# Reading a third row block's normalised input back transposed, with its layer-norm sums on ScalarE, in a linear-attention block kernel

## Chip, core and metric

The kernel runs on one NeuronCore of a Trainium2 chip. The metric is the device time of one execution in microseconds (us); smaller is better. The core has five engines that matter here: TensorE (PE in the profile, with its weight loads as PEld), VectorE (DVE), ScalarE (ACT), GpSimd (POOL) and SyncE (SP, which only issues DMAs). Each engine takes its instructions strictly in the order in which the kernel wrote them, and waits on semaphores for the others.

## What is computed

One transformer block on 2048 rows of 512 numbers, with a conditioning vector `c`:

```python
mod = (silu(c) @ w_mod).reshape(1, 6, 1, 512)
sa, ca, ga, sb, cb, gb = (mod[:, i] for i in range(6))
h = layernorm(x) * (1 + ca) + sa
q, k, v = h @ wqkv                 # 32 heads of 16
pq, pk = phi(q), phi(k)            # phi(t) = where(t > 0, t + 1, exp(t)) + 1e-6
kv, z = pk^T v, sum of pk over the rows
x = x + ga * ((pq kv) / (pq z + 1e-6)) @ wo
h = layernorm(x) * (1 + cb) + sb
x = x + gb * (mish(h @ w1 + b1) @ w2)
```

Only the first layer norm and the K products, in the first fifth of the program, are touched by the change.

## The kernel before, in words

**Tiling.** The 2048 rows are four blocks (b = 0 to 3) of four tiles (t = 0 to 3) of 128 rows by 512 columns. All tensors are float32; each product is made of three matmuls of split numbers: a tile is cut into an upper part (`...h`, type fp32r) and the rest (`...l`), and `mm3` (lines 76 to 78) multiplies upper by upper, upper by rest and rest by upper. `split` (lines 80 to 94) writes the upper part with a copy on ScalarE (line 84) or GpSimd (line 86) and the rest with a subtraction on VectorE (line 90, or 92 with a constant added).

**One block of the first stage.** Each block is loaded (`load_x`), its layer norm is taken (mean and variance per row, then `x` is normalised in place), and from then on two forms of it are used. Normalised rows, split, are `xn`. The transposed block, scaled and shifted by the modulation columns `mc` and split, is `hT` (four tiles, j = 0 to 3, of 128 columns by 512 rows). `k_unit(b, t)` multiplies `hT` of the block by the K weights into `pk`, 12 matmuls; `k_post` makes `phi` of it (`e_k` and `relu_k` on ScalarE, `ku` on VectorE) and splits that into `pk...h` (ScalarE) and `pk...l` (VectorE). `g_unit(b, t)` then adds the product of `xn` and `pk` to `gacc`, 12 matmuls. So TensorE has, for each block from b = 1, four k units and then four g units, and the next block's `hT` has to be there when the g units end.

**How hT is made.** Block 2 and block 1 go through TensorE: `transpose` (line 277) makes four transposes of 128x128 for each of the four `hT` tiles into PSUM, ScalarE scales and shifts them into `hf` (line 287), then `split`. Block 3, the only one in `TURNED`, goes through memory instead: the normalised tiles are written to DRAM (`to_dram`, line 243, on GpSimd's queue), are read back in squares of 32 rows (`load_squares`, line 256, 16 DMAs on SyncE's queue), each 128x512 tile is turned by a VectorE transpose in `turn` (line 264), and ScalarE scales and shifts it in SBUF (line 269).

**How the layer norm is made.** `ln_side` (line 487) takes the statistics of all four tiles of a block on VectorE (`bn_stats` and `bn_aggr`, lines 198 and 199), one tile per step; `ln_rstd` raises variance + eps to the power -1/2 on GpSimd (line 207); tiles 0 and 1 are then normalised on ScalarE (line 216) and tiles 2 and 3 on VectorE (line 218). A second way exists for single tiles of blocks 0 and 1: `act_sums` (line 220) gets mean and sum of squares with two ScalarE instructions that accumulate along the row (lines 228 and 229).

**The order of the work** is written by hand. The main program calls the units in TensorE's order; generators given to `spawn` are advanced one step by each `tick()`, generators given to `spawn_idle` when their turn comes, at most two a tick. What a step issues is appended to the queue of its engine at that point, and stays there. `q_right(c)` (idle work, line 386) makes the differences `qt` of blocks 0 and 1 for a later product: eight subtractions, eight upper and eight rest parts. `mod_side` multiplies modulation weights `wm` on VectorE. `tick` follows every unit, so in block 1 there are eight ticks, in block 2 eight more.

Of the kernel before, what the change touches and what calls it, by code (L numbers as in the profile page):

```python
# [11 lines left out]
ALU = mybir.AluOpType  # L12

P = 128
S = 2048
D = 512
F = 1792
NB = S // 512
NF = F // P
LAG = 3  # L20

TURNED = (3,)
SLOTS = 101
EPS = 1e-5
TINY = 1e-6
# [2 lines left out]
def block_kernel(ctx: ExitStack, tc: tile.TileContext, x, wqkv, wo, w1, b1t, w2, c, wmodt, out):  # L28
# [23 lines left out]
    def spawn(gen):  # L52
        fresh.append(iter(gen))
# [44 lines left out]
    def load_x(b, j, key="x", eng=sp):  # L98
        t = xt[key, b, j] = sb(f"{key}_{b}_{j}")
        r0 = 512 * b + P * j  # L100
        eng.dma_start(t, x[r0:r0 + P, :])
# [90 lines left out]
    def ln_stats(key, b, j, t):  # L192

        for d, name, shape in (mv, "mv", [P, 4, 2]), (rs, "rs", [P, 4]), (nb, "nb", [P, 4]):
            if (key, b) not in d:
                d[key, b] = cst.tile(shape, F32, tag=name, name=f"{name}_{key}_{b}", bufs=NB)
        st6 = cst.tile([P, 6], F32, tag="st6", name=f"st6_{key}_{b}_{j}", bufs=4)
        dve.bn_stats(st6, t)
        dve.bn_aggr(mv[key, b][:, j, :], st6)

    def ln_eps(key, b, lo=0, hi=4):
        dve.tensor_scalar(rs[key, b][:, lo:hi], mv[key, b][:, lo:hi, 1], EPS, 1.0, op0=ALU.add, op1=ALU.mult)  # L202

    def ln_rstd(key, b, lo=0, hi=4):

        y = rs[key, b][:, lo:hi]
        pool.tensor_tensor(y, y, half[:, lo:hi], op=ALU.pow)  # L207

    def ln_shift(key, b, lo=0, hi=4):

        dve.scalar_tensor_tensor(nb[key, b][:, lo:hi], mv[key, b][:, lo:hi, 0], -1.0, rs[key, b][:, lo:hi],
                                 op0=ALU.mult, op1=ALU.mult)
# [28 lines left out]

    nd, yd = {}, {}

    def to_dram(key, b, t, v):
        if (key, b) not in nd:
            nd[key, b] = drp.tile([512, D], F32, name=f"{key}d_{b}")
        pool.dma_start(nd[key, b][P * t:P * (t + 1), :], v)

    def squares(y, d, col):

# [233 lines left out]
                        plus_one(16, 20)  # L484
            yield

    def ln_side(b):
        for j in range(4):
            ln_stats("x", b, j, xt["x", b, j])
            if j == 3:  # L490
                ln_eps("x", b)
                ln_rstd("x", b)
            yield
        ln_shift("x", b)
        for j in range(4):
            t = xt["x", b, j]
            ln_apply("x", b, j, t, t, act if j < 2 else dve)
            if j % 2:
                yield
                if b in TURNED:  # L500
                    for i in (j - 1, j):
                        to_dram("x", b, i, xt["x", b, i])


    def stats(b, t):
        ln_stats("x", b, t, xt["x", b, t])
# [140 lines left out]
    apply(1, 3, act, shift=False)  # L647
    step(xsplit[3], kpost[3])
    make_constants()
    for j in range(4):  # L650
        load_x(2, j)
    g_unit(0, 2)
    spawn(ln_side(2))
    tick()
    for j in range(4):
        tr = transpose("x", 1, j, 4, 0, "h" if j < 3 else "tp", pool)
# [175 lines left out]
    for b in range(1, NB):  # L832
        last = b == NB - 1
        if b == NB - 2:
            spawn(mod_side(range(8, 12), 1))
        for t in range(4):
            k_unit(b, t)
            if b + 2 < NB:
                load_x(b + 2, t)
                if b + 2 in TURNED and t == 2:  # L840
                    spawn(ln_side(b + 2))
            if b + 1 in TURNED and t == 3:
                load_squares("x", b + 1, range(4))
            if b == NB - 2:
                load_wqkv(0, t)
            if last and t < 2:
                spawn_idle(q_left(t))
            if last and t == 2:
                spawn_idle(early_rows[0])
            xn_split(b, t)  # L850
            tick()
        if b + 2 < NB and b + 2 not in TURNED:
            spawn(ln_side(b + 2))
        if last:
            spawn(wo_scale())
        for t in range(4):
            if b + 1 in TURNED and t < 2:
                for j in (2 * t, 2 * t + 1):
                    tr = turn_x(b + 1, j)
                    next(tr)  # L860
                    spawn(tr)
            elif not last and b + 1 not in TURNED and t % 2 == 0:
                for j in (t, t + 1):
                    tr = transpose("x", b + 1, j, 4, 0, "tp" if j == t else "h")
                    next(tr)
                    spawn(tr)
            g_unit(b, t)
            if b == 1 and t == 1:
                spawn_idle(q_right(0))
            if b == 1 and t == 3:  # L870
                spawn_idle(q_right(1))
            if last:
                load_x(0, t, "r")
                for k in ((0, 1), (2,), (3,), ())[t]:
                    spawn(split(f"wq_{k}", wraw[0, k], wq, k))
                if t == 2:
                    z_unit()
                if t == 3:
                    spawn(z_side())
            if b == NB - 2:  # L880
                wv[t] = sb(f"wv_{t}")
                sp.dma_start(wv[t], wqkv[P * t:P * (t + 1), 1024:1536])
                wos[t] = sb(f"wo_{t}")
                sp.dma_start(wos[t], wo[P * t:P * (t + 1), :])
            tick()
# [669 lines left out]
```

## Time and profile before

| what | value |
| --- | --- |
| time, median of 3 runs | 485.33 us (484.69 to 486.44) |
| span of the profiled execution, first to last instruction | 483.0 us |
| what lies around the span: median less span | 2.3 us (the lowest and the highest run: 1.7 and 3.4) |
| PE busy | 477.7 us, 99% |
| DVE busy | 384.5 us, 80% |
| ACT busy | 295.7 us, 61% |
| POOL busy | 148.4 us, 31% |
| granted TensorE clock | 1.000 |

The profiled execution has no device time of its own on record apart from its span, so the 2.3 us around it come from the median of the three timed runs. In the timeline a row reads: start, duration, engine, line, operation, tiles written and read, shape, count, and in brackets how long the engine had been idle before it and what ended that. Two instructions of one engine overlap a little in their rows, so what an instruction costs its queue is the distance from its start to the next start, not its duration.

### The profile page before, as it was taken

Reading aid. Unit: us, or ns where it says so; the run is one execution under the profiler, and the core shown is the slowest. Engines: PE = TensorE matmul, PEld = TensorE weight load, DVE = VectorE, ACT = ScalarE, POOL = GpSimd, SP = SyncE. Lnnn points to the kernel's source line nnn. Section 1 sums busy time; section 2 is a strip of 40 time slices with the busy share of each in tenths; the row PEclk is TensorE's granted clock in tenths of the full one; section 3 lists DMA queues with packets and bytes.
Section 4 is the critical chain, followed back from the end, with each engine's and each line's share of the span. In section 5 each row is a group of like instructions: output and inputs, shape, how many; then the busy total and the mean of one; then the engine's idle time right before and its main releaser. Section 6 shows DMA issues by size and latency. Waiting matters only on the chain.

```text
span 483.0 us, 7291 instructions
## 1 busy us (share of the span) xinstructions
PE 477.7 (99%) x2342; PEld 393.6 (81%) x2342; DVE 384.5 (80%) x741; ACT 295.7 (61%) x528; POOL 148.4 (31%) x248
## 2 busy tenths in 40 slices
PE   8999999999999999999999999999999999999997
PEld 6788887878878888888888888888888888888887
DVE  7989989999799699977775874899644664789993
ACT  6777686866555979647676755683174454668300
POOL 4583320000022114102324434323617410243500
PEclk9999999999999999999999999999999999999999
DMA  8805599144874307389699998979999922499977
GB/s 312 299 9 127 138 160 266 51 135 150 290 196 110 121 30 263 111 284 335 216 299 350 364 251 187 321 227 340 346 363 332 291 61 62 109 181 211 240 117 167
DMA packets 121823, 101.69 MB, mean 211 GB/s; under 512 B 65937, under 2 KB 87449, under 8 KB 121786
## 3 DMA queue, kind: packets, MB, share of 16 engines
q1 hardware_dynamic: 90504, 55.47, 41.2%
q0 software_dynamic: 29024, 45.24, 37.3%
q10 hardware_dynamic: 2258, 0.53, 0.5%
q8 instruction: 18, 0.29, 0.3%
q14 instruction: 19, 0.16, 0.1%
HBM read 64.50 MB, written 34.61 MB: 205 GB/s over the span
## 4 chain that ended last, share of the span: by engine, by line
PE 93%; DVE 4%; ACT 1%; issue 1%; POOL 0%; ACTq 0%; DVEq 0%
PE p_a L1142 20%; PE p_s L1142 8%; PE oacc L78 5%; PE oacc L76 5%; PE oacc L77 5%; PE m L78 5%; PE m L77 5%; PE m L76 5%; PE o L76 3%; PE o L78 3%; PE o L77 3%; PE pq_a L409 3%; PE pk L78 2%; PE pk L76 2%; PE pk L77 2%; PE gacc L77 2%
## 5 line engine op out<-in xcount | busy, mean ns | idle before, releaser
L207 POOL TENSOR_TENSOR rs_n<-rs_n,half 128x1 f32<-128x1 f32 x16 | 11.4, 711 | 62.0 <-DVE rs_n L202 36.4
L1147 DVE TENSOR_TENSOR cb<-p_s,u 128x512 f32<-128x512 f32 x28 | 19.2, 687 | 11.6 <-ACT u L1183 10.9
L1152 ACT ACTIVATE u<-p_a 128x512 f32<-128x512 f32 x14 | 8.4, 598 | 26.2 <-PE p_a L1142 17.9
L1440 POOL DMA_DIRECT2D wt_m<-w2t x20 | 14.0, 702 | 32.9 <-PE p_a L1142 21.4
L1134 ACT ACTIVATE ub<-cb,b1c 128x512 f32<-128x512 f32 x28 | 20.0, 717 | 5.6 <-DVE cb L1147 5.4
L1177 ACT ACTIVATE u<-p_a 128x512 f32<-128x512 f32 x12 | 7.2, 599 | 24.7 <-PE p_a L1142 24.7
L1183 ACT ACTIVATE u<-p_a 128x512 f32<-128x512 f32 x14 | 8.4, 597 | 15.7 <-PE p_a L1142 15.7
L1147 DVE TENSOR_TENSOR c<-p_a,u 128x512 f32<-128x512 f32 x14 | 9.5, 688 | 8.2 <-PE p_a L1142 7.1
L900 POOL DMA_DIRECT2D rden_d<-rden x2 | 1.4, 719 | 46.5 <-DVE rden L898 46.5
L300 ACT ACTIVATE e_k<-pk 128x512 f32<-128x512 f32 x15 | 8.9, 591 | 10.8 <-PE pk L78 10.8
L779 POOL DMA_DIRECT2D w2b<-w2d x20 | 10.6, 541 | 14.5 <-DVE r L1126 4.6
L773 POOL DMA_DIRECT2D wb<-w2d x14 | 9.9, 709 | 12.4 <-DVE t L751 10.7
L303 DVE SCALAR_TENSOR_TENSOR ku<-e_k,relu_k 128x512 f32<-128x512 f32 x15 | 10.7, 713 | 3.1 <-ACT relu_k L301 3.1
L1111 ACT ACTIVATE u<-p_a,b1c 128x512 f32<-128x512 f32 x14 | 9.6, 684 | 5.4 <-PE p_a L1142 5.4
L303 DVE SCALAR_TENSOR_TENSOR q<-e_q,relu_q 128x512 f32<-128x512 f32 x16 | 10.7, 687 | 2.7 <-ACT relu_q L301 2.7
L207 POOL TENSOR_TENSOR rs_x<-rs_x,half 128x1 f32<-128x1 f32 (+1 forms) x10 | 7.7, 780 | 15.8 <-DVE rs_x L202 14.6
L312 POOL DMA_DIRECT2D ku<-ku x8 | 7.2, 898 | 16.5 <-DVE ku L303 16.5
L826 POOL DMA_DIRECT2D a1b<-rd_a x10 | 5.4, 540 | 21.1 <-DVE b_1l L90 9.6
L924 DVE TENSOR_TENSOR r<-o,r 128x512 f32<-128x512 f32 x16 | 10.9, 680 | 0.9 <-PE o L78 0.9
L719 DVE TENSOR_TENSOR w2r<-w2r,gb_bc 128x512 f32<-128x512 f32 x14 | 9.1, 686 | 2.7 <-DMA w2r<-in_w_dram 2.7
L912 DVE SCALAR_TENSOR_TENSOR q<-q,rd 128x512 f32<-128x512 f32 x16 | 10.5, 689 | 0.5 <-DMA rd<-rden_d 0.5
L929 POOL DMA_DIRECT2D x1d<-r x8 | 4.4, 546 | 20.9 <-DVE r L924 20.9
(1617 smaller groups left out, 1892.6 us busy)
## 6 DMA issues: line engine op xcount, KB each, us to landing
wm<-in_wmodt_dram SPq DMA_DIRECT2D x24, 256.0 KB, 5.4
w2b<-w2d POOLq DMA_DIRECT2D x20, 256.0 KB, 6.3
wt_m<-w2t POOLq DMA_DIRECT2D x20, 256.0 KB, 6.0
r<-in_x_dram SPq DMA_DIRECT2D x16, 256.0 KB, 3.5
x<-in_x_dram SPq DMA_DIRECT2D x15, 256.0 KB, 4.8
w1p<-in_w_dram SPq DMA_DIRECT2D x14, 256.0 KB, 4.1
w2r<-in_w_dram SPq DMA_DIRECT2D x14, 256.0 KB, 6.2
wb<-w2d POOLq DMA_DIRECT2D x14, 256.0 KB, 5.4
```

The costliest lines, as they stand in the source:

```text
L76: pe.matmul(o, st[0], mv[0], start=start, stop=False)
L77: pe.matmul(o, st[0], mv[1], start=False, stop=False)
L78: pe.matmul(o, st[1], mv[0], start=False, stop=stop)
L207: pool.tensor_tensor(y, y, half[:, lo:hi], op=ALU.pow)
L303: dve.scalar_tensor_tensor(dst, e, 1.0, r, op0=ALU.min, op1=ALU.add)
L409: pe.matmul(p, l, r, start=onto is None and c == 0 and i == 0, stop=c == 1 and i == 2, skip_group_check=onto is not None)
L779: pool.dma_start(w2s[f][i], w2d[f // 2, i][:, f % 2, :])
L924: dve.tensor_tensor(r, p, r, op=ALU.add)
L1134: act.activation(u, p, AF.Mish, bias=b1c[:, f:f + 1])
L1142: pe.matmul(p, st, mv, start=onto is None and c == 0 and i == 0, stop=c == 1 and i == 2, skip_group_check=onto is not None)
L1147: dve.tensor_tensor(out, p, u, op=ALU.add)
L1440: pool.dma_start(v, w2t[g][:, :, SUM[name], :])
```

## The change

Block 2 joins block 3 in `TURNED`: its 16 TensorE transposes go, and its normalised tiles are written to DRAM, on SyncE's queue, read back in squares and turned on VectorE. `ln_side` is replaced by `ln_turned(b, on_act, per, queue)`: `on_act` tiles get their sums from `act_sums` on ScalarE and are normalised on ScalarE, the rest stays on VectorE; `per` is the number of tiles in a step. Block 2 has two tiles on ScalarE, block 3 all four. The loads of block 3 are written right behind those of block 2, the layer norm of block 3 is spawned at k unit 1 of block 1 (before: unit 2), the turns are done at g units 1 and 2 (before: 0 and 1), and `q_right(0)` starts one unit later.

```diff
-TURNED = (3,)
+TURNED = (2, 3)
...
-    def to_dram(key, b, t, v):
+    def to_dram(key, b, t, v, queue=pool):
         if (key, b) not in nd:
             nd[key, b] = drp.tile([512, D], F32, name=f"{key}d_{b}")
-        pool.dma_start(nd[key, b][P * t:P * (t + 1), :], v)
+        queue.dma_start(nd[key, b][P * t:P * (t + 1), :], v)
...
-    def ln_side(b):
-        for j in range(4):
-            ln_stats("x", b, j, xt["x", b, j])
-            if j == 3:
-                ln_eps("x", b)
-                ln_rstd("x", b)
-            yield
-        ln_shift("x", b)
-        for j in range(4):
-            t = xt["x", b, j]
-            ln_apply("x", b, j, t, t, act if j < 2 else dve)
-            if j % 2:
+    def ln_turned(b, on_act, per, queue):
+
+        sums = {}
+        rest = list(range(on_act, 4))
+        for n in range(max(on_act, len(rest))):
+            if n < on_act:
+                sums[n] = act_sums("x", b, n, xt["x", b, n])
+            if n < len(rest):
+                ln_stats("x", b, rest[n], xt["x", b, rest[n]])
+            if (n + 1) % per == 0:
                 yield
-                if b in TURNED:
-                    for i in (j - 1, j):
-                        to_dram("x", b, i, xt["x", b, i])
-
+        for n in range(on_act):
+            dve.tensor_scalar(rs["x", b][:, n:n + 1], sums[n][:, 1:2], 1.0 / D, EPS, op0=ALU.mult, op1=ALU.add)
+        if rest:
+            ln_eps("x", b, on_act, 4)
+        ln_rstd("x", b)
+        yield
+        for n in range(on_act):
+            sums_shift("x", b, n, sums[n])
+        for pair in (0, 2), (1, 3):
+            for j in pair:
+                ln_apply("x", b, j, xt["x", b, j], xt["x", b, j], act if j < on_act else dve)
+            if per == 1:
+                yield
+            for j in pair:
+                to_dram("x", b, j, xt["x", b, j], queue)
+        if b == 2:
+            yield
+            load_squares("x", b, range(4))
...
-    for j in range(4):
-        load_x(2, j)
+    for b in (2, 3):
+        for j in range(4):
+            load_x(b, j)
     g_unit(0, 2)
-    spawn(ln_side(2))
+    spawn(ln_turned(2, 2, 2, sp))
     tick()
...
             k_unit(b, t)
-            if b + 2 < NB:
-                load_x(b + 2, t)
-                if b + 2 in TURNED and t == 2:
-                    spawn(ln_side(b + 2))
-            if b + 1 in TURNED and t == 3:
-                load_squares("x", b + 1, range(4))
+            if b == 1 and t == 1:
+                spawn(ln_turned(3, 4, 1, pool))
+            if b == 2 and t == 3:
+                load_squares("x", 3, range(4))
...
-            if b + 1 in TURNED and t < 2:
-                for j in (2 * t, 2 * t + 1):
+            if b + 1 in TURNED and t in (1, 2):
+                for j in (2 * t - 2, 2 * t - 1):
                     tr = turn_x(b + 1, j)
...
-            if b == 1 and t == 1:
+            if b == 1 and t == 2:
                 spawn_idle(q_right(0))
```

The built programs show what stands where. In their rows the first number of a name is the tile (j or t) and the last one a buffer; the block is not in the name. The first place is **ScalarE's queue at the end of the prologue**, between the normalising of block 1 (line 216) and the first K tile of block 1 (`e_k`). Before:

```order
L216 ACTIVATE x_3_110<-x_3_110,nb_x_334,rs_x_333 128x512
L287 ACTIVATE hf_x_0_468<-tp_x_0_463,mc 128x512
L287 ACTIVATE hf_x_1_478<-tp_x_1_473,mc 128x512
L287 ACTIVATE hf_x_2_488<-tp_x_2_483,mc 128x512
L287 ACTIVATE hf_x_3_498<-tp_x_3_493,mc 128x512
L300 ACTIVATE e_k_0_544<-pk_0_525 128x512
```

and now:

```order
L216 ACTIVATE x_3_110<-x_3_110,nb_x_334,rs_x_333 128x512
L228 ACTIVATE scrap_x_0_467,sums_x_0_468<-x_0_437 128x512
L229 ACTIVATE scrap_x_0_467,sums_x_0_468<-x_0_437,sums_x_0_468 128x512
L228 ACTIVATE scrap_x_1_475,sums_x_1_476<-x_1_439 128x512
L229 ACTIVATE scrap_x_1_475,sums_x_1_476<-x_1_439,sums_x_1_476 128x512
L287 ACTIVATE hf_x_0_487<-tp_x_0_482,mc 128x512
L287 ACTIVATE hf_x_1_497<-tp_x_1_492,mc 128x512
L287 ACTIVATE hf_x_2_507<-tp_x_2_502,mc 128x512
L287 ACTIVATE hf_x_3_517<-tp_x_3_512,mc 128x512
L216 ACTIVATE x_0_437<-x_0_437,nb_x_466,rs_x_465 128x512
L216 ACTIVATE x_1_439<-x_1_439,nb_x_466,rs_x_465 128x512
L300 ACTIVATE e_k_0_570<-pk_0_545 128x512
```

The sums of two tiles of block 2 stand ahead of block 1's four `hf`, and the normalising of these two tiles ahead of block 1's first `e_k`.

The second place is **ScalarE's queue in the g units of block 1**, from the last K tile of block 1 to the last `hT` of block 2 (`hT_x_3h`). Before:

```order
L84 ACTIVATE xn_3h<-x_3_110 128x512
L287 ACTIVATE hf_x_0_663<-tp_x_0_658,mc 128x512
L84 ACTIVATE hT_x_0h<-hf_x_0_663 128x512
L287 ACTIVATE hf_x_1_673<-tp_x_1_668,mc 128x512
L84 ACTIVATE hT_x_1h<-hf_x_1_673 128x512
L84 ACTIVATE pk_3h<-ku_3_650 128x512
L287 ACTIVATE hf_x_2_732<-tp_x_2_727,mc 128x512
L84 ACTIVATE hT_x_2h<-hf_x_2_732 128x512
L287 ACTIVATE hf_x_3_742<-tp_x_3_737,mc 128x512
L84 ACTIVATE hT_x_3h<-hf_x_3_742 128x512
```

and now:

```order
L228 ACTIVATE scrap_x_3_705,sums_x_3_706<-x_3_451 128x512
L229 ACTIVATE scrap_x_3_705,sums_x_3_706<-x_3_451,sums_x_3_706 128x512
L84 ACTIVATE pk_3h<-ku_3_685 128x512
L269 ACTIVATE hf_x_0_716<-hf_x_0_716,mc 128x512
L84 ACTIVATE hT_x_0h<-hf_x_0_716 128x512
L269 ACTIVATE hf_x_1_718<-hf_x_1_718,mc 128x512
L84 ACTIVATE hT_x_1h<-hf_x_1_718 128x512
L216 ACTIVATE x_0_445<-x_0_445,nb_x_621,rs_x_620 128x512
L216 ACTIVATE x_2_449<-x_2_449,nb_x_621,rs_x_620 128x512
L269 ACTIVATE hf_x_2_747<-hf_x_2_747,mc 128x512
L84 ACTIVATE hT_x_2h<-hf_x_2_747 128x512
L269 ACTIVATE hf_x_3_749<-hf_x_3_749,mc 128x512
```

The sums of block 3's last tile are now ahead of `pk_3h` and of all of block 2's `hf` (the other three pairs of sums stand among the k tiles before them), and the normalising of tiles 0 and 2 of block 3 stands between the second and the third `hT`.

The third place is **VectorE's queue from the last `hT` of block 2 on**, where the differences `qt` stand ahead of block 2's first K tile (`ku`). Before:

```order
L90 TENSOR_TENSOR hT_x_3l<-hf_x_3_742,hT_x_3h 128x512
L391 TENSOR_TENSOR qt_2_723<-hf_x_2_488,hf_x_0_468 128x512
L391 TENSOR_TENSOR qt_3_724<-hf_x_2_277,qt_1_722 128x512
L218 TENSOR_SCALAR x_2_597<-x_2_597,mv_x_614,rs_x_615 128x512
L218 TENSOR_SCALAR x_3_636<-x_3_636,mv_x_614,rs_x_615 128x512
L391 TENSOR_TENSOR qt_0_786<-hf_x_1_478,hf_x_1_245 128x512
L391 TENSOR_TENSOR qt_1_787<-hf_x_3_498,qt_0_786 128x512
L90 TENSOR_TENSOR qt_0l<-qt_0_721,qt_0h 128x512
L391 TENSOR_TENSOR qt_2_788<-hf_x_3_498,hf_x_1_478 128x512
L391 TENSOR_TENSOR qt_3_789<-hf_x_3_294,qt_1_787 128x512
L303 SCALAR_TENSOR_TENSOR ku_0_811<-e_k_0_812,relu_k_0_813 128x512
```

and now:

```order
L90 TENSOR_TENSOR hT_x_2l<-hf_x_2_747,hT_x_2h 128x512
L90 TENSOR_TENSOR hT_x_3l<-hf_x_3_749,hT_x_3h 128x512
L391 TENSOR_TENSOR qt_2_781<-hf_x_2_507,hf_x_0_487 128x512
L391 TENSOR_TENSOR qt_3_782<-hf_x_2_277,qt_1_780 128x512
L391 TENSOR_TENSOR qt_0_806<-hf_x_1_497,hf_x_1_245 128x512
L391 TENSOR_TENSOR qt_1_807<-hf_x_3_517,qt_0_806 128x512
L391 TENSOR_TENSOR qt_2_808<-hf_x_3_517,hf_x_1_497 128x512
L391 TENSOR_TENSOR qt_3_809<-hf_x_3_294,qt_1_807 128x512
L303 SCALAR_TENSOR_TENSOR ku_0_831<-e_k_0_832,relu_k_0_833 128x512
```

The six subtractions still stand behind `hT_x_3l`; the normalising of two tiles of block 3 (line 218) has gone from between them to ScalarE, and the first rest part (`qt_0l`) behind `ku`. From `hT_x_3l` of block 2 to the `pk_3l` of block 2 the new queue has 25 operations of 128x512 (each reading two tensors), three `wm` products with accumulation, two transposes, and then `pk_3l` itself.

2 lines of the change are left out of this document (removed).

## The prediction

> **What bounds the kernel now.** First the page: the busy shares and the chain that ended last.
>
> ```profile
> span 483.0 us, 7291 instructions
> PE 477.7 (99%) x2342; PEld 393.6 (81%) x2342; DVE 384.5 (80%) x741; ACT 295.7 (61%) x528; POOL 148.4 (31%) x248
> PE 93%; DVE 4%; ACT 1%; issue 1%; POOL 0%; ACTq 0%; DVEq 0%
> ```
>
> TensorE is the bound: whatever leaves its queue is gained, and whatever makes it wait is lost, one for one. Over the whole span ScalarE looks free (61%). The change acts between 30 and 85 us, so next comes the view of busy time by stretch, there alone (columns: stretch; sum; then PE, PEld, DVE, ACT and POOL, each with its count; clock; DMA share; GB/s).
>
> ```profile
> 41.00:47.00 6.00, 6.00 (x32) 5.02 (x31) 5.54 (x11) 5.61 (x11) 2.28 (x4) 1.00 0.76 165
> 47.00:53.00 6.00, 6.00 (x32) 4.99 (x30) 5.62 (x13) 4.66 (x9) 0.52 (x1) 1.00 0.56 144
> 53.00:59.00 6.00, 6.00 (x32) 5.03 (x31) 5.42 (x11) 4.65 (x7) 3.90 (x5) 1.00 0.37 87
> 59.00:62.00 3.00, 3.00 (x15) 2.49 (x14) 2.96 (x5) 0.09 (x1) 0.81 (x2) 1.00 0.71 262
> 70.00:78.00 8.00, 8.00 (x37) 6.64 (x36) 8.00 (x17) 5.88 (x11) 1.71 (x2) 1.00 1.06 232
> ```
>
> From 41 to 62 us (block 1's units) ScalarE is busy 15.0 of 21 us, so it has 6.0 us left; VectorE is full, and from 70 to 78 us (block 2) it has nothing left at all. Last, the waits of TensorE's weight loads between 22 and 106 us, the two that touch this chain:
>
> ```profile
> PEld gacc L77 <- DVE pk_3l L92: 0.6, 1, 0.6
> PEld pk L78 <- DVE hT_x_2l L90: 0.2, 1, 0.2
> ```
>
> So there are two places without slack already: block 1's first k unit waits for `hT` made in the prologue, and block 2's last g unit waits 0.6 us for VectorE's `pk_3l`.
>
> **The gain.** Two pieces of the chain are the 16 transposes that go:
>
> ```profile
> 46.46 0.87 PE tp_x L281 x8
> 52.81 0.88 PE tp_x L281 x8
> ```
>
> That is **-1.75 us** on TensorE.
>
> **ScalarE in the prologue.** ScalarE's sums for block 2's tiles 0 and 1 now stand ahead of block 1's four `hf`. Their price, and what waits behind:
>
> ```profile
> 25.62 0.65 ACT L228 ACTIVATE scrap_x<-x 128x512 f32<-128x512 f32 x1
> 27.12 2.21 ACT L216 ACTIVATE x<-x,nb_x,rs_x 128x512 f32<-128x512 f32 x3
> 29.88 0.82 ACT L216 ACTIVATE x<-x,nb_x,rs_x 128x512 f32<-128x512 f32 x1 [0.55 <-DVE nb_x L237]
> 31.52 2.79 ACT L287 ACTIVATE hf_x<-tp_x,mc 128x512 f32<-128x512 f32 x4 [0.83 <-PE tp_x L281]
> 33.30 0.61 POOL L86 CAST hT_x_0h<-hf_x 128x512 fp32r<-128x512 f32 x1
> 35.43 1.07 POOL L86 CAST hT_x_3h<-hf_x 128x512 fp32r<-128x512 f32 x1
> 36.97 0.68 DVE L90 TENSOR_TENSOR hT_x_3l<-hf_x,hT_x_3h 128x512 fp32r<-128x512 f32 x1
> 37.18 0.42 PE L78 MATMUL pk<-wk_2h,hT_x_2l 128*128 128x512 f32 x1
> ```
>
> One tile's sums (two accumulating passes and their read-outs) hold ScalarE from 25.62 to 27.12, 1.50 us; two cost 3.0. The fourth normalising starts at 29.88 and needs some 0.7, so `hf` starts at 33.6 instead of 31.52, 2.1 us late. GpSimd hides part of that: its cast of `hT_x_0h` stood behind the making of constants on that queue and began at 33.30, 1 us after `hf` was there; now it waits for the first `hf`, done at 33.6 + 0.8 = 34.4: 1.1 us late. The second `hf` comes 0.7 behind the first, while the casts followed at 0.55, so the later tiles are some 1.2 late. The matmul on `hT_x_2l` waited for its operand already, so TensorE waits **+1.2 us** more in block 1's first k unit (at least 0.9, if contention of the casts with VectorE eases; at most 2.1, the whole delay).
>
> **ScalarE in block 1.** This is the term that decides. What leads into it:
>
> ```profile
> 39.55 1.47 POOL L207 TENSOR_TENSOR rs_x<-rs_x,half 128x4 f32<-128x4 f32 x1 [3.05 <-DVE rs_x L202]
> 38.33 0.60 ACT L300 ACTIVATE e_k<-pk 128x512 f32<-128x512 f32 x1 [4.02 <-PE pk L78]
> 38.82 0.59 ACT L301 ACTIVATE relu_k<-pk 128x512 f32<-128x512 f32 x1
> 39.30 0.63 ACT L84 ACTIVATE xn_0h<-x 128x512 fp32r<-128x512 f32 x1
> 42.54 1.51 ACT L216 ACTIVATE x<-x,nb_x,rs_x 128x512 f32<-128x512 f32 x2
> 43.95 0.62 ACT L84 ACTIVATE pk_1h<-ku 128x512 fp32r<-128x512 f32 x1
> 75.46 0.80 ACT L269 ACTIVATE hf_x<-hf_x,mc 128x512 f32<-128x512 f32 x1
> 76.83 0.80 ACT L269 ACTIVATE hf_x<-hf_x,mc 128x512 f32<-128x512 f32 x1
> 55.43 0.63 ACT L84 ACTIVATE hT_x_3h<-hf_x 128x512 fp32r<-128x512 f32 x1
> ```
>
> ScalarE's next instructions, the normalising of block 2's tiles 0 and 1, need the power on GpSimd, which stands behind the four casts. These now end at 35.43 + 1.07 + 1.2 = 37.7; the power takes 1.47: 39.2; VectorE's shift: 39.5. From there I lay the queue end to end, by distances between starts: two normalisings 1.4 (42.54 to 43.95), so `e_k` starts at 40.9, not 38.33. Then four tiles of `e_k` 0.49, `relu_k` 0.48, `xn` 0.52 and `pk` 0.52 are 8.0; block 3's four pairs of sums 4 x 1.50 = 6.0; a wait for `ku` in the first tile some 0.4: 55.3. Two pairs of `hf` and `hT` at 1.37 (75.46 to 76.83): 58.0. Block 3's normalising of tiles 0 and 2 needs the second power, behind the last sums and VectorE's turns: wait 0.4, then 1.4: 59.8. Two more pairs 2.74: 62.6. So `hT_x_3h` of block 2 is done at about **62.7** (before: 56.06), and its rest part 0.7 later, 63.4. TensorE ended this k unit at 61.72 before (the next unit's first row, below); now its last matmul can't start before 63.5. The 6.0 us that ScalarE had left are filled to the last by the 6.0 of the sums, and it enters 2.6 us late.
>
> **VectorE in block 2.** Its queue saved six statistics, but what it has to do behind `hT_x_3l` can't start earlier than that operand.
>
> ```profile
> 59.00 0.39 PE L76 MATMUL pk<-wk_0h,hT_x_0h 128*128 128x512 f32 x1
> 61.72 0.39 PE L76 MATMUL pk<-wk_0h,hT_x_0h 128*128 128x512 f32 x1
> 66.36 0.68 DVE L90 TENSOR_TENSOR xn_1l<-x,xn_1h 128x512 fp32r<-128x512 f32 x1
> 68.17 0.69 DVE L183 SCALAR_TENSOR_TENSOR wm<-wm,sc_row 128x512 f32<-128x512 f32 x1
> 68.78 0.69 DVE L92 SCALAR_TENSOR_TENSOR pk_1l<-ku,pk_1h 128x512 fp32r<-128x512 f32 x1
> 71.80 1.30 DVE L267 STREAM_TRANSPOSE hf_x<-y_x 128x512 f32<-128x512 f32 x2
> 73.02 0.64 DVE L183 SCALAR_TENSOR_TENSOR wm<-wm,sc_row 128x512 f32<-128x512 f32 x1
> 77.85 0.68 DVE L92 SCALAR_TENSOR_TENSOR pk_3l<-ku,pk_3h 128x512 fp32r<-128x512 f32 x1
> ```
>
> Three plain operations take from 66.36 to 68.17, so 0.603 each; a `wm` 0.61; a pair of transposes 1.22. From `hT_x_3l` to `pk_3l` the new queue has 25 x 0.603 + 3 x 0.61 + 1.22 = 18.1 us without a pause that I can find (`ku` of the first tile comes up at 67, while ScalarE, behind two more normalisings from 62.6 on, has done its `e_k` and `relu_k` by 65.2). 62.75 + 18.1: `pk_3l` runs at 80.9 and is done at 81.5; before it was done at 78.53. TensorE, from 63.7 on, needs it at 63.7 + 6 x 2.72 + 0.2 = 80.2 (a unit is 12 matmuls, 59.00 to 61.72, with three k units and three g units in between), so it waits there, as before, and this place ends **3.0 us later**. The turned `hT` of block 3 follow as closely as before: `hT_x_0l` is done at about 84.6, and is wanted at 84.5: +0.1.
>
> **The sum.** By TensorE: -1.75 for the transposes, +1.2 in block 1's first unit, about +2.5 in block 1's last g unit and block 2's first k unit together, +1.1 more at `pk_3l`: +3.1. Behind 85 us TensorE has no wait to take this back in, and its queue is unchanged, so the span goes from 483.0 to 486.1, and with the 2.3 us around it the time to **488.4 us**. (The 2.3 are the median of the runs less the span, so the sum stands on the median as well.) The sums' own bound: were their 1.50 wrong by 0.2 each, four of them move the end by 0.8 either way; the pauses that I put at 0.8 in all may be nothing or 2.
>
> **A rule that speaks for the change.** The Trainium skill, Perfetto Trace Analysis, section "Identifying the Most-Contended Engine", says to find the engine with the highest occupancy and to optimize that one first; here that is TensorE, and relief for it at ScalarE's cost should pay, which would give the first rival below. By the stretches above, ScalarE's 61% is an average over stages, and in the one stage touched it has just the 6.0 us that the sums ask for; I go by the stretch.
>
> **The rivals.**
>
> 1. *Faster: ScalarE keeps up.* If ScalarE's queue is shorter than I lay it, TensorE keeps the 1.75 us: 483.6. It decides by when `hT_x_3h` of block 2 is done: with no other wait TensorE wants it at some 60 us, so ScalarE must be 2.7 us faster than 62.7, which the sums alone would give at 0.8 us each instead of 1.50; VectorE's queue then starts and ends earlier by the same, and its place at `pk_3l` with it. For it speaks ScalarE's idle time before 38.33 (4.02 us, part of which the prologue's sums take), against it that every duration comes from this trace. Chance 0.13.
> 2. *A wash.* Only the prologue's wait is real and block 1's queue ends in time: -1.75 + 1.2 = -0.5, so 484.8. Against it the same end-to-end sum. Chance 0.08.
> 3. *Slower still: the memory path.* The transfers of both blocks:
>
> ```profile
> 62.13 9.32 SPq L262 DMA_DIRECT2D y_x<-xd  x16
> y_x<-xd SPq DMA_DIRECT2D x16, 64.0 KB, 3.3
> wm<-in_wmodt_dram SPq DMA_DIRECT2D x24, 256.0 KB, 5.4
> ```
>
> Block 2's tiles can be written from 40.4 to 42 and are read from about 45 to 54; with 3.3 us to land the last square is there at 57.5, and `hf` of tile 2 asks at 58.4, so there is a little slack. The weight loads that stand behind these 20 DMAs on SyncE's queue go out from 54 and are first read by the first `wm` on VectorE, at about 70 (68.17 before), which hides them. Block 3's last tiles are normalised only behind `hT_x_3h`, at 64; their squares go out from about 67 to 76, and the last `wm`, behind them in SyncE's queue at about 77, lands at 82.4, 1 us before VectorE reads it ahead of `hT_x_0l`. If either is 3 us later than its median, TensorE waits 2 us more: 490.4. The Trainium skill, DMA: Bandwidth & Descriptors, section "Why small descriptors are slow (HBM only)", says that each packet has a fixed overhead, which weighs most on small ones; the squares' rows are such, and their 9.32 us is how the trace shows it. Chance 0.10.
>
> My forecast has the remaining 0.69.
>
> **How the numbers follow.** A measurement of this kernel can tell about 0.3%, 1.5 us, from no change. Faster by more: rival 1, 0.13. Within: rival 2, 0.08. Slower by more: forecast and rival 3, 0.79. The range leaves rival 1 out, and the far end of rival 3. Its low end, 485.6, is the forecast less the pauses and less 0.2 us on each sum, with a part of the wash; its high end, 490.4, is the forecast with pauses of 2 us in all and the sums at 1.7.
>
> **What would show it.** Right: TensorE without the 16 transposes; a wait of about 1 us for `hT_x_2l` or its neighbours near 37 us; ScalarE without a pause over 0.5 us from 39.5 to 64; waits for `hT_x_2h` to `hT_x_3l` of block 2 near 62; `pk_3l` of block 2 done near 81.5. Wrong: `hT_x_3h` of block 2 done before 60.5, VectorE with pauses between 63 and 81, or TensorE waiting for anything behind a DMA.

## The result, and the profile after

The changed kernel takes **487.8 us** (median; 487.12 to 487.84), against 485.33 us before. The ratio is **1.0048, 95% interval 1.0034 to 1.0061**: slower by some 2.3 us. The forecast was 488.4 us, slower by 3.1. The page of the changed kernel, its busy shares and the chain that ended last:

```profile
span 486.1 us, 7325 instructions
PE 477.5 (98%) x2326; PEld 390.8 (80%) x2326; DVE 382.2 (79%) x740; ACT 305.9 (63%) x554; POOL 148.0 (30%) x248
PE 87%; DVE 5%; DMA 2%; ACT 2%; SPq 2%; issue 1%; POOL 1%; DVEq 0%; ACTq 0%
```

TensorE has 16 instructions fewer, and yet 6% of the span has left it on the chain: it now passes through VectorE, a DMA, ScalarE and SyncE's queue. The same stretches as before, same columns:

```profile
41.00:47.00 6.00, 6.00 (x28) 4.98 (x27) 2.92 (x5) 5.73 (x13) 1.98 (x2) 1.00 0.83 229
47.00:53.00 6.00, 6.00 (x28) 4.97 (x27) 3.03 (x5) 5.93 (x15) 0.85 (x1) 1.00 0.98 159
53.00:59.00 6.00, 6.00 (x27) 4.66 (x26) 5.09 (x16) 5.66 (x12) 2.27 (x2) 1.00 0.97 212
59.00:62.00 3.00, 2.10 (x10) 1.35 (x8) 2.74 (x5) 2.97 (x5) 1.14 (x2) 1.00 0.96 247
70.00:78.00 8.00, 8.00 (x37) 6.64 (x36) 8.00 (x16) 7.62 (x16) 1.73 (x3) 1.00 1.17 189
```

ScalarE went from 15.0 to 20.3 of 21 us, VectorE from 11.2 to 6.0 of the 12 us from 41 to 53, the DMA engines from 0.37 to 0.97 of their time between 53 and 59 us. TensorE waits where the forecast put it; its weight loads' waits from 22 to 106 us:

```profile
PEld gacc L77 <- DVE pk_3l L92: 2.0, 2, 1.6
PEld pk L76 <- ACT hT_x_2h L84: 1.3, 1, 1.3
PEld pk L78 <- DVE hT_x_2l L90: 0.9, 2, 0.5
PEld pk L78 <- DVE hT_x_1l L90: 0.8, 1, 0.8
PEld pk L76 <- ACT hT_x_3h L84: 0.5, 1, 0.5
```

The chain of waits between 54 and 63 us (start, duration, what; "x2" are two instructions) shows by which way `hT_x_3h` of block 2 comes:

```profile
54.86 2.91 DMA y_x<-xd
57.85 0.20 DVE hf_x L267
58.49 0.13 DVE nb_x L237
58.64 1.52 ACT x L216 x2
60.17 0.72 ACT hf_x L269
60.91 0.63 ACT hT_x_2h L84
61.54 0.72 ACT hf_x L269
62.28 0.64 ACT hT_x_3h L84
```

Before, TensorE itself carried this stretch of the chain. Now the last of block 2's squares lands at 57.8, VectorE turns it, only then does its in-order queue reach block 3's shift `nb_x`, and ScalarE normalises two tiles of block 3 ahead of block 2's last two `hf`.

For the rest of this section and the next one measure serves: the end of TensorE's last matmul of each stage, read from the timelines, as the difference from the kernel before, each stage less the stage ahead of it. The first number is less the difference that was there already when block 0's k units ended, ahead of anything changed (+0.48 us in this profile, from -0.27 to +0.88 in the others: chance). All in us:

| kernel | prologue and block 1's k units | block 1's g | block 2's k | block 2's g | block 3's first two k | sum | timed ratio, 95% interval |
| --- | --- | --- | --- | --- | --- | --- | --- |
| the change | +1.26 | -1.56 | +2.16 | +1.05 | +0.04 | +2.95 | 1.0048 [1.0034, 1.0061] |
| sums alone | +1.23 | +0.95 | 0.00 | +0.07 | +0.07 | +2.32 | 1.0053 [1.0041, 1.0065] |
| block 3: two tiles on ScalarE | +1.26 | -1.82 | +3.54 | +0.96 | +0.01 | +3.95 | 1.0065 [1.0050, 1.0080] |
| block 3: none on ScalarE | +1.26 | -1.82 | +2.43 | +0.91 | +0.07 | +2.85 | 1.0061 [1.0048, 1.0074] |
| block 2: none on ScalarE | +0.32 | -1.82 | +1.37 | +1.07 | +0.16 | +1.10 | 1.0016 [1.0008, 1.0025] |
| turn alone | +1.28 | -1.79 | +2.15 | +0.96 | +0.10 | +2.70 | 1.0036 [1.0024, 1.0049] |
| `q_right(1)` late | +1.28 | -1.59 | +2.18 | -0.46 | +1.64 | +3.05 | 1.0118 [1.0102, 1.0134] |
| block 3: two tiles, later | +1.25 | -1.82 | +2.54 | +0.92 | +0.09 | +2.98 | 1.0045 [1.0033, 1.0058] |
| block 2: none, and block 3: two, later | +0.36 | -1.82 | +1.68 | +0.92 | +0.07 | +1.21 | 1.0017 [1.0008, 1.0026] |
| normalising behind | +1.28 | -1.55 | +0.88 | +0.94 | +0.31 | +1.86 | 1.0029 [1.0017, 1.0041] |
| that, and block 2 on VectorE | +0.27 | -1.82 | +0.09 | +0.95 | +0.47 | -0.04 | 1.0002 [0.9992, 1.0013] |
| that, and `q_right(0)` early | +0.26 | -1.82 | +1.31 | -0.46 | +4.17 | +3.46 | 1.0045 [1.0029, 1.0062] |
| that, with rest parts on GpSimd | +0.34 | -1.82 | +0.74 | +3.80 | +0.36 | +3.42 | 1.0031 [1.0018, 1.0044] |

### The profile page after: what moved, and what is told of

Read it like the earlier page. It is cut to its first block, busy times and chain, and to the rows that moved or that the text cites. A ratio compares the mean times of both kernels' runs of the same rounds, so it can differ in the third digit from the quotient of the medians.

```text
span 486.1 us, 7325 instructions
## 1 busy us (share of the span) xinstructions
PE 477.5 (98%) x2326; PEld 390.8 (80%) x2326; DVE 382.2 (79%) x740; ACT 305.9 (63%) x554; POOL 148.0 (30%) x248
## 4 chain that ended last, share of the span: by engine, by line
PE 87%; DVE 5%; DMA 2%; ACT 2%; SPq 2%; issue 1%; POOL 1%; DVEq 0%; ACTq 0%
PE p_a L1151 20%; PE p_s L1151 8%; PE oacc L76 5%; PE oacc L78 5%; PE oacc L77 5%; PE m L77 5%; PE m L76 5%; PE m L78 5%; PE o L76 3%; PE o L78 3%; PE o L77 3%; PE pq_a L409 3%; PE pq L76 2%; PE pq L78 2%; PE pq L77 1%; PE pk L78 1%
## 5 line engine op out<-in xcount | busy, mean ns | idle before, releaser
L216 ACT ACTIVATE x<-x,nb_x,rs_x 128x512 f32<-128x512 f32 x13 | 10.0, 808 | 4.6 <-DVE nb_x L237 3.9
L183 DVE SCALAR_TENSOR_TENSOR wm<-wm,sc_row 128x512 f32<-128x512 f32 x16 | 10.6, 681 | 0.0
```

The source lines that it names most:

```text
L183: dve.scalar_tensor_tensor(t, t, 1.0, row, op0=ALU.mult, op1=ALU.mult, accum_out=mc[:, i:i + 1])
```

## The experiments

The theory on record (A): the sums fill ScalarE's queue in block 1, so block 2's last `hT` come late. Against it stood the memory path (B), which the chain above names. The first four runs each take one part away.

### The sums alone

```diff
-TURNED = (2, 3)
+TURNED = (3,)
```

with the store and the squares only for blocks in `TURNED`; block 2 goes through TensorE's transposes again.

> One part alone: the layer-norm sums of blocks 2 and 3 stand on ScalarE as in the change, but block 2 keeps its 16 TensorE transposes, so nothing of block 2 goes through device memory. Theory A (ScalarE's queue sets block 2's first k unit): hT_x_3h of block 2 still comes at about 62 to 63 us, since the sums are ahead of it just as before; the 1.75 us of transposes only fill part of TensorE's waits there, so the time is that of the changed kernel, 487.3 to 488.3. Theory B (the way through device memory is what is late: the squares land at 57.8 us and VectorE's nb_x of block 3 stands behind them): with no squares ScalarE runs on, hT_x_3h comes before 61 us, and only the 1.2 us of the prologue is lost, 486 to 487.

Measured: 487.83 us, 1.0053. The time is A's, but not by A's way. `hT_x_3h` of block 2 came at 60.2, in time, and block 2's k units lost nothing. With the transposes kept, the +0.95 is lost a unit earlier; ScalarE's row, and the waits between 48 and 64 us:

```profile
59.60 0.63 ACT L84 ACTIVATE hT_x_3h<-hf_x 128x512 fp32r<-128x512 f32 x1
PEld gacc L76 <- ACT pk_3h L84: 0.6, 1, 0.6
PEld gacc L77 <- DVE pk_3l L92: 0.5, 1, 0.5
```

ScalarE, full of sums, is late with block 1's `pk_3h`. So the sums cost 2.2 us (+1.23 and +0.95) with nothing gained for them. B was right that `hT_x_3h` comes before 61 us without the squares, and wrong that only the prologue's loss would remain.

### Block 3's sums taken off ScalarE, half and whole

```diff
-                spawn(ln_turned(3, 4, 1, pool))
+                spawn(ln_turned(3, 2, 1, pool))
```

> The change with two instead of four of block 3's tiles summed and normalised on ScalarE (the other two on VectorE): 3.0 us of sums and 0.76 us of normalising fewer stand in ScalarE's queue ahead of hT_x_3h of block 2. Theory A (ScalarE's queue): hT_x_3h comes near 59.5 us instead of 62.9, the waits in block 2's first k unit (about 2.3 us) go, 485.0 to 486.3. Theory B (memory): ScalarE's normalising still starts at 58.6 behind VectorE's turning of squares that land at 57.8, hT_x_3h is earlier by only the 0.76 us, 486.8 to 487.6.

The other run has 0 in place of 2:

> The change with all of block 3's layer norm on VectorE: 6.0 us of sums and 3.0 us of normalising leave ScalarE. Theory A: no wait for ScalarE is left in block 2's first k unit; VectorE takes some 6 us of statistics more, of which the half-idle stretch from 41 to 53 us hides most; 484.5 to 486.5, and what is left over the kernel before is the prologue's 1.2. Theory B (memory): block 2's squares land no earlier, hT_x_2h and its neighbours wait for VectorE's turning, 486 to 487.5. If VectorE is the bound, its pk_3l of block 2 comes after 82 us and the time is 488 or more.

The tiles whose sums leave ScalarE are normalised on VectorE as well. Measured: 488.41 us (1.0065), above both ranges, and 488.14 us (1.0061), which only the third case of that run allowed; neither is faster than the change. With two tiles, VectorE and then ScalarE stand and wait for a square (timelines of VectorE, ScalarE and TensorE):

```profile
59.40 0.71 DVE L267 STREAM_TRANSPOSE hf_x<-y_x 128x512 f32<-128x512 f32 x1 [3.59 <-DMA y_x<-xd]
60.15 0.82 ACT L269 ACTIVATE hf_x<-hf_x,mc 128x512 f32<-128x512 f32 x1 [2.34 <-DVE hf_x L267]
60.74 0.50 PE L78 MATMUL pk<-wk_0h,hT_x_0l 128*128 128x512 f32 x1 [1.96 <-DVE hT_x_0l L90]
```

ScalarE was relieved, and idle for 2.34 us. The square landed at 59.4 instead of 57.8, although its issues ended earlier (54.5 against 55.4). The profile is of the execution that took 489.37 us; the six took from 486.68 to 489.37, so a part of this may be that one's own. In this kernel block 3's tiles are normalised, and stored on GpSimd's queue, while the squares are under way. With all on VectorE its own queue is late: the normalising of block 3's last two tiles stands ahead of `hT_x_2l`.

```profile
61.79 1.00 DVE L218 TENSOR_SCALAR x<-x,mv_x,rs_x 128x512 f32<-128x512 f32 x2
62.70 0.68 DVE L90 TENSOR_TENSOR hT_x_2l<-hf_x,hT_x_2h 128x512 fp32r<-128x512 f32 x1
63.44 0.50 PE L78 MATMUL pk<-wk_2h,hT_x_2l 128*128 128x512 f32 x1 [1.79 <-DVE hT_x_2l L90]
```

In both, TensorE waits for VectorE's parts instead of ScalarE's. A as the whole cause of block 2's k units falls.

### Block 2's sums taken off ScalarE

```diff
-    spawn(ln_turned(2, 2, 2, sp))
+    spawn(ln_turned(2, 0, 4, sp))
```

> The change with block 2's statistics on VectorE in place of two tiles' sums on ScalarE (block 3's four stay on ScalarE): 2.9 us less ScalarE work ahead of block 1's hf in the prologue. Prologue term: the 1.2 us that TensorE waits in block 1's first k unit goes. Theory A: ScalarE enters block 1 about 2.9 us earlier, so hT_x_3h of block 2 comes near 60 and most of the 2.3 us there goes as well, 484.5 to 486. Theory B (memory): the squares still land near 57.8, so only the prologue's 1.2 goes, less what VectorE's statistics cost in the prologue: 486.3 to 487.3.

The two tiles are normalised on VectorE as well. Measured: 485.85 us, 1.0016, inside A's range. That does not decide for A, because B's premise did not hold either (squares still near 57.8 us; the last one was turned from 55.40 on). The prologue's term goes from +1.26 to +0.32, and block 2's k units lose 1.37 instead of 2.16: with the prologue everything starts earlier, the squares too. SyncE's queue in the change and here:

```profile
44.88 10.48 SPq L262 DMA_DIRECT2D y_x<-xd  x16
```

```profile
42.52 10.63 SPq L262 DMA_DIRECT2D y_x<-xd  x16
```

The two sums in the prologue are the dearest single part of the change: taking them away gives back 0.0032 of the time, 1.6 us (difference of the two ratios, each to the kernel before timed beside it).

### The turn alone, and block 3's two tiles begun later

These test a third theory (C): several chains end within 2 us of each other. In the first run `ln_side` of the kernel before serves block 3, from k unit 2; in the second block 3's `ln_turned` is spawned two units later.

```diff
-            if b == 1 and t == 1:
-                spawn(ln_turned(3, 4, 1, pool))
+            if b == 1 and t == 2:
+                spawn(ln_side(3))
```

> The other part alone: block 2 as in the change, block 3's layer norm as before it (statistics on VectorE, two tiles normalised on each engine, begun one k unit later). The earlier two relief runs left a third theory, C: block 2's first k unit is bounded by several chains that end within 2 us of each other, ScalarE's queue, VectorE's queue and the landing of the squares, so taking work off one of them only hands the end to the next. Theory A (ScalarE's queue alone): 485 to 486.3, with hT_x_3h before 61. Theory C: VectorE's statistics and its normalising stand ahead of its low parts, or block 3's store to device memory delays the last squares; TensorE waits for hT_x_0l to hT_x_3l instead, 487.3 to 488.6.

```diff
-            if b == 1 and t == 1:
-                spawn(ln_turned(3, 4, 1, pool))
+            if b == 1 and t == 3:
+                spawn(ln_turned(3, 2, 1, pool))
```

> Like the run with two of block 3's tiles on ScalarE, but block 3's layer norm begun two k units later (after block 1's last k unit), so that its store to device memory does not run beside block 2's squares and only one of its normalising steps stands ahead of the high parts on ScalarE. Theory A (ScalarE's queue): with 3.0 us of sums fewer and no contention, hT_x_3h comes near 60 and the time is 485.3 to 486.5. Theory C (chains of nearly equal length): the squares still land at 57.8, VectorE's two statistics stand right ahead of its turning, and only about 0.5 to 1 us of the 2.3 comes back, 486.6 to 487.6.

Measured: 487.21 us (1.0036) and 487.56 us (1.0045). ScalarE's timeline at that place, turn alone first, then the later start:

```profile
57.88 1.52 ACT L216 ACTIVATE x<-x,nb_x,rs_x 128x512 f32<-128x512 f32 x2 [2.29 <-DMA wr<-in_wqkv_dram]
61.51 0.63 ACT L84 ACTIVATE hT_x_3h<-hf_x 128x512 fp32r<-128x512 f32 x1
```

```profile
58.36 0.81 ACT L216 ACTIVATE x<-x,nb_x,rs_x 128x512 f32<-128x512 f32 x1 [2.31 <-DVE nb_x L237]
61.28 0.63 ACT L84 ACTIVATE hT_x_3h<-hf_x 128x512 fp32r<-128x512 f32 x1
```

ScalarE stands idle for 2.3 us in both, and goes on only when `nb_x` comes, behind the last square (57.1 and 57.6 on VectorE; the releaser in the first row is a load that ended at that time, while in VectorE's timeline `nb_x` runs at 57.73). That is C: with the sums away, the squares' chain sets the end at almost the same time. In the change itself ScalarE waited 0.25 us for `nb_x`: the two chains are that close. The later start did remove the late square of the two-tile run (+3.54 to +2.54).

### `q_right(1)` late

VectorE's chain from `hT_x_3l` to `pk_3l` of block 2 was the forecast's last term. Here the eight operations of `q_right(1)`, seven of which stood in that chain, are moved behind it.

```diff
-            if b == 1 and t == 3:
+            if b == 2 and t == 3:
                 spawn_idle(q_right(1))
```

> The change with q_right(1) (four subtractions and four splits, 8 VectorE operations of 0.6 us and 4 of ScalarE's) started after block 2's last g unit instead of block 1's; nothing else moved. If VectorE's unbroken chain from hT_x_3l to pk_3l of block 2 is what sets the third block's last g unit, pk_3l is done 4 us earlier, near 78, the waits of 1.6 and 0.4 us for it go, and the time falls by 1.1 to 2.0: 485.8 to 486.8. If block 3's squares (landing up to 79.2 us, turned ahead of pk_3l) are the next limit right behind, pk_3l is done near 80.5 to 81 and the time falls by 0.3 to 0.8 only. VectorE is also full from 88 to 112 us in the changed kernel, so the 4.8 us come back there: if TensorE waits for them, the gain is lost, 487.3 to 488.3.

Measured: 491.42 us, 1.0118, a miss: no case allowed more than 488.3. At the place itself the step is right: `pk_3l` ran at 77.38 (81.21 in the change) and block 2's g units gained 0.46 instead of losing 1.05. But it came back behind it; VectorE's timeline, and the waits of TensorE's weight loads from 84 to 140 us:

```profile
80.28 0.71 DVE L267 STREAM_TRANSPOSE hf_x<-y_x 128x512 f32<-128x512 f32 x1 [1.52 <-DMA y_x<-xd]
83.30 0.69 DVE L183 SCALAR_TENSOR_TENSOR wm<-wm,sc_row 128x512 f32<-128x512 f32 x1 [2.31 <-DMA wm<-in_wmodt_dram]
```

```profile
PEld pq_s L409 <- DVE cq L420: 2.0, 1, 2.0
PEld pk L78 <- DVE hT_x_0l L90: 1.7, 1, 1.7
PEld z L359 <- DVE ku L310: 1.6, 1, 1.6
```

The loss in block 3's first k units (+1.64) is not VectorE's work: VectorE stands idle there, for 1.52 us until block 3's last square has landed, and for 2.31 us until a `wm` load has landed that stands behind the squares on SyncE's queue. In the change VectorE comes to that `wm` at 83.64 us, and the load, issued 0.5 us earlier than here (77.84 against 78.33), would have landed at some 82.8 (an estimate from the 4.97 us that it took here). So a shorter chain on VectorE can bring block 3's `hT_x_0l` forward by less than 1 us. Behind that VectorE is full (busy for all of 92 to 100 us), and some 4.5 us more were lost in the profile, about the 4.8 that were moved; 1.5 us had been gained.

### Block 2 on VectorE and block 3 later

The edit of block 2 from above with the later start of block 3's two tiles.

> Block 2's statistics on VectorE (as in the run that took 485.85 us) and block 3's two-and-two split begun two k units later. With all of block 1 some 2.3 us earlier, the squares land near 55.4 and hT_x_3h can come near 58. Theory A and C agree on the direction: TensorE's waits in block 2's first k unit (2.2 us there) shrink to under 1, and 484.3 to 485.3 is expected; if pk_3l of block 2 then still comes near 79 us, TensorE waits there for what it won, and the time stays at 485.5 to 486.

Measured: 486.07 us, 1.0017, just above the second range and no better than block 2's edit alone (1.0016): relief for ScalarE buys nothing there, even with the squares issued from 42.7 us on.

### The normalising behind `hT_x_3h`

If the chain runs from the last square over `nb_x` and two normalisings to `hf`, it is enough to change the order. One step more of waiting:

```diff
         ln_rstd("x", b)
         yield
+        if b == 3:
+            yield
         for n in range(on_act):
             sums_shift("x", b, n, sums[n])
```

> The change with one step of waiting more in block 3's layer norm, so that its shift on VectorE and its first two normalisings on ScalarE (1.5 us) stand behind hT_x_3h of block 2 and not between the tiles 1 and 2; sums, squares and all else stay. Theory D, formed from the runs so far: the high parts of tiles 2 and 3 wait for one chain, the last square's landing (57.8 us), VectorE's nb_x behind it, then the two normalisings in ScalarE's order; so hT_x_2h and hT_x_3h come 1.4 us earlier (61.5 for the second), the waits of 1.3 and 0.5 us shrink, and the time is 486.2 to 486.9. Theory A in its first form (the sums fill ScalarE's queue) gives the same 1.4 us, and only the trace can part them: ScalarE must then have no pause before tile 2's scaling. If VectorE's low parts are the limit right behind, 487.2 to 488.

Measured: 486.45 us, 1.0029, inside the first range. All sums stay, and ScalarE goes from `hT_x_1h` to tile 2 without a pause; its timeline, and VectorE's:

```profile
57.79 0.63 ACT L84 ACTIVATE hT_x_1h<-hf_x 128x512 fp32r<-128x512 f32 x1
58.33 0.80 ACT L269 ACTIVATE hf_x<-hf_x,mc 128x512 f32<-128x512 f32 x1
60.53 0.64 ACT L84 ACTIVATE hT_x_3h<-hf_x 128x512 fp32r<-128x512 f32 x1
61.65 0.69 DVE L90 TENSOR_TENSOR hT_x_3l<-hf_x,hT_x_3h 128x512 fp32r<-128x512 f32 x1
```

`hT_x_3h` begins 1.75 us earlier than in the change (62.28), and block 2's k units lose 0.88 instead of 2.16: the order alone was worth 1.3 us in the profile, and by the ratios 0.9 us (their intervals overlap). What is left is VectorE's, whose `hT_x_3l` stands behind two `qt`. By itself this run does not part ScalarE's full queue from the chain over `nb_x`, since the step takes 1.4 us out of both: ScalarE now runs without a pause up to `hT_x_3h`, as A asked. What parts them are the turn alone and the later start, in which ScalarE, with sums taken off, stood idle until `nb_x` came.

### Towards a faster kernel

Three runs combine what helped. Block 2 on VectorE and the normalising behind:

> Both at once: block 2's statistics on VectorE (prologue term gone, block 1 some 2.3 us earlier; 485.85 us by itself) and block 3's normalising behind hT_x_3h (about 1.2 us by theory D). 484.4 to 485.2. If pk_3l of block 2 is then the limit again (its wait grows by what the seam gives), 485.4 to 486.

Measured: 485.16 us against 484.93 for the kernel before timed beside it, at the upper end of the first range, 1.0002 [0.9992, 1.0013]: the kernel before, to within what can be told. Block 2's k units lose 0.09; the 1.82 us of the transposes are there, and go again at `pk_3l` (wait 1.5 us, +0.95), with +0.47 and +0.27 at the ends. To shorten that chain, `q_right(0)` is begun earlier, with its upper parts on GpSimd:

```diff
+            if b == 1 and t == 1:
+                spawn_idle(q_right(0))
             xn_split(b, t)
...
-            if b == 1 and t == 2:
-                spawn_idle(q_right(0))
...
-            yield from split(f"qt_{c}_{i}", t[i], qb, (f"t{i + 1}", c))
+            yield from split(f"qt_{c}_{i}", t[i], qb, (f"t{i + 1}", c), hi_engine=pool if c == 0 else act)
```

> As the run before, and q_right(0) (8 VectorE operations of 0.6 us) started in block 1's second k unit, where VectorE is half idle, instead of its third g unit; its high parts on GpSimd. VectorE's chain from hT_x_3l to pk_3l of block 2 is 3 to 4 us shorter, so if that chain sets the third block's last g unit its 1.5 us wait goes: 483.2 to 484.4, faster than the kernel before. If block 3's squares are the limit right behind (turned ahead of pk_3l and for block 3's first k unit), the gain stops near 484.8 to 485.4.

Measured: 487.09 us, 1.0045, a miss. The wait for `pk_3l` is gone (-0.46). But VectorE, early now, waits for block 3's squares, and TensorE behind it (VectorE's and TensorE's timelines, and TensorE's stretch behind the pause):

```profile
80.59 0.71 DVE L267 STREAM_TRANSPOSE hf_x<-y_x 128x512 f32<-128x512 f32 x1 [2.14 <-DMA y_x<-xd]
83.19 0.50 PE L78 MATMUL pk<-wk_0h,hT_x_0l 128*128 128x512 f32 x1 [2.26 <-DVE hT_x_0l L90]
84.00:86.00 2.00, 2.00 (x7) 1.51 (x6) 1.97 (x6) 0.00 (x0) 0.00 (x0) 0.50 0.99 357
```

The pause was 2.26 us, and the granted clock fell to 0.50 behind it, which made the loss 4.17. The clock is not the whole of it: three of the six executions had a mean granted clock of 1.000, and these took 486.12 to 486.39 us, still more than the kernel before. Block 2's k units lose 1.31 as well: VectorE's `hT_x_0l` took 1.75 us instead of 0.69 beside GpSimd's casts of the upper parts, and TensorE waited 0.7 us for it and 0.9 for `hT_x_2l`. The last run leaves the order as it was and gives the four rest parts of `q_right(1)` to GpSimd:

```diff
-            yield from split(f"qt_{c}_{i}", t[i], qb, (f"t{i + 1}", c))
+            yield from split(f"qt_{c}_{i}", t[i], qb, (f"t{i + 1}", c), lo_engine=pool if c == 1 else dve)
+            if c == 1:
+                yield
```

> As the run with block 2 on VectorE and block 3's normalising behind hT_x_3h (485.16 us), and the four low parts of q_right(1) subtracted on GpSimd instead of VectorE, one per step as before: 3 operations of 0.6 us leave VectorE's chain ahead of pk_3l of block 2, nothing else is moved and no squares are moved. If that chain is the limit there, pk_3l comes 1.8 us earlier, its 1.5 us wait goes and the time is 483.4 to 484.6, faster than the kernel before. If block 3's squares and the mod weights behind them are the limit right behind (block 3's first k unit then waits for hT_x_0l instead), 484.6 to 485.4. If GpSimd's subtraction (1.3 us for such a tile in the profile before) holds up VectorE beside it, 485.4 to 487.

Measured: 487.08 us, 1.0031; its third case, and more. GpSimd's and VectorE's timelines, and TensorE's:

```profile
68.32 2.08 POOL L90 TENSOR_TENSOR qt_0l<-qt,qt_0h 128x512 fp32r<-128x512 f32 x1 [5.30 <-ACT qt_0h L84]
69.18 1.78 DVE L92 SCALAR_TENSOR_TENSOR pk_1l<-ku,pk_1h 128x512 fp32r<-128x512 f32 x1
77.90 1.29 DVE L267 STREAM_TRANSPOSE hf_x<-y_x 128x512 f32<-128x512 f32 x2
78.05 1.26 POOL L90 TENSOR_TENSOR qt_3l<-qt,qt_3h 128x512 fp32r<-128x512 f32 x1 [1.02 <-ACT qt_3h L84]
80.53 0.50 PE L77 MATMUL gacc<-pk_3l,xn_3h 128*128 128x512 f32 x1 [2.38 <-DVE pk_3l L92]
82.00:84.00 2.00, 2.00 (x7) 1.52 (x6) 2.00 (x5) 1.94 (x4) 0.00 (x0) 0.50 1.06 353
```

Three of the four subtractions on GpSimd held up the VectorE operation beside them (`pk_1l`, `xn_2l` and a `ku`) from 0.68 to 1.78 us; the fourth ran beside two transposes, which took no longer. So VectorE's chain from `hT_x_3l` to `pk_3l` became longer, 19.85 us instead of 18.27 in the run before last, although three of its operations were gone. `pk_3l` ran at 79.79 against 77.09; the other 1.1 us are a later `hT_x_3l`. No version that was run beats the kernel before.

## Why the prediction was right, step by step

- **The gain, -1.75.** Shown: block 1's g units are 1.82 us shorter wherever nothing waits in them.
- **The prologue, +1.2.** Shown, +1.26, and +1.23 to +1.28 in every run with block 2's sums on ScalarE; +0.26 to +0.36 without. Two tiles' sums held ScalarE 2.92 us, 3.0 expected:

```profile
31.10 0.62 ACT L228 ACTIVATE scrap_x<-x 128x512 f32<-128x512 f32 x1
34.02 2.77 ACT L287 ACTIVATE hf_x<-tp_x,mc 128x512 f32<-128x512 f32 x4
37.82 0.50 PE L78 MATMUL pk<-wk_1h,hT_x_1l 128*128 128x512 f32 x1 [0.38 <-DVE hT_x_1l L90]
```

- **Block 1's end and block 2's first k unit, +2.5.** The size is right: +2.16 and, in block 1's g units, 0.26 (-1.56 less -1.82), so 2.42; `hT_x_3h` was done at 62.9, 62.7 expected. The reason given was half of it. "The 6.0 us that ScalarE had left are filled to the last by the 6.0 of the sums" nearly holds (20.3 of 21 us), but the sums do not decide alone: with them gone from block 3 nothing came back. A second chain, the last square's landing, VectorE's turn, `nb_x` and the two normalisings, ends within 0.25 us of ScalarE's own queue:

```profile
58.64 1.52 ACT L216 ACTIVATE x<-x,nb_x,rs_x 128x512 f32<-128x512 f32 x2 [0.25 <-DVE nb_x L237]
```

  So the size is no luck, as ScalarE's queue alone would have ended there too; what the prediction missed is that relief for ScalarE would bring nothing. It had the parts (a wait of 0.4 for VectorE's turns, 1.4 of normalising, a little slack at the square) and did not say that they would hold the end by themselves; it named TensorE waiting behind a DMA as a sign of being wrong, and that sign is there.
- **VectorE's chain, +1.1.** Shown, +1.05. From the start of `hT_x_3l` to the start of `pk_3l` it took 18.27 us (62.94 to 81.21), 18.1 expected, without a pause as expected, and the term was +0.91 to +1.07 in every run that turned block 2 and left the chain alone; it changed sign in the two runs that shortened it.

```profile
62.94 0.69 DVE L90 TENSOR_TENSOR hT_x_3l<-hf_x,hT_x_3h 128x512 fp32r<-128x512 f32 x1 [0.68 <-ACT hT_x_3h L84]
81.21 0.69 DVE L92 SCALAR_TENSOR_TENSOR pk_3l<-ku,pk_3h 128x512 fp32r<-128x512 f32 x1
```

- **The sum.** +2.95 by stages, +3.1 forecast. The span of 486.1 is the forecast's to the digit, partly by luck: it holds the 0.48 us of late start, and some 0.3 came back at the program's end. The timed difference, 2.3 us, is 0.8 below the forecast.
- **The rivals.** ScalarE did not keep up, and the wash did not come. The memory path was priced as 2 us on top; it is a limit beside ScalarE's, and comes out alone when ScalarE is relieved. At block 3 it did not bind in the change, but it does when VectorE comes there sooner (`q_right(1)` late). The 9.32 us that the prediction reads as the sign of small packets are the time in which SyncE's queue issued the 16 DMAs; what the small rows have to do with it, no run separates.

Still open: why the last square landed 1.6 us later in the two-tile run. That block 3's store ran beside it is argued from the order, and the run that began later bears it out, but it also moved VectorE's and ScalarE's work, and each run has one profile. Faster squares by themselves were not tried.

## What to carry to other kernels

Ask of the stage, not of the span, how much time an engine has left: ScalarE at 61% had 6.0 us in the stage touched, and 5.3 of them were used. When a relieved engine stands idle at the old place and the time stays, a second chain ends there too; in an in-order queue the cheapest cure may be to put the instruction that waits behind those that do not, here worth about 1 us for one step. And moving work off one wait can only move the wait: 4.8 us of VectorE's work, moved behind, gained 1.5 us and cost some 5, at a DMA first and then on a VectorE without idle time.

## What the hardware showed beside that

**The clock.** In the profiled executions TensorE's pauses of 1.20 (the change), 1.79 and 1.96 us (block 3's sums taken off ScalarE) left the granted clock at 1.00. The two pauses of 2.26 and 2.38 us were followed, 0.5 and 1.2 us after the start of the first matmul, by stretches at 0.50, with matmuls 0.43 us apart instead of 0.23 for some 3.4 us. The Trainium skill, TensorE: Matmul & The Clock Gate, section "Why this matters for your kernels", advises against gaps over about 3 us; here 2.26 could already be too long, and the measurement decides. The kernel does not settle it, however: a stretch of 3.4 us at 0.50 lowers the mean clock of these spans to some 0.996, and of the six executions of the run with 2.26 three had 0.996 (487.79 to 488.68 us) and three 1.000 (486.12 to 486.39), of the eleven of the run with 2.38 six and five. Two of the five executions of the run with 1.79 had 0.996 too, and one of the five of the turn alone, whose profile has no pause over 1.14 there. What parts them is open, since each run has one profile.

**GpSimd beside VectorE.** The rows of the last run, 0.68 us stretched to 1.78 by a GpSimd subtraction that began first, agree with the Trainium skill, SBUF — State Buffer, section "SBUF: two separate sides": the two engines share a pair of ports, and a VectorE operation with two inputs in SBUF waits for a GpSimd operation that reads SBUF to end. The two transposes that were not held up (1.29 us for both, beside 1.26 us of GpSimd) read one tensor each.
